# Asking for the next pair's norms before the first row chunk, and binding its transpositions behind scores, in the first batch of an attention and spectral-FFN kernel

## The chip, the cores and the metric

The kernel runs on one core of a Trainium2 chip. The metric is the time of one execution on the device in microseconds (us). The engines named below are TensorE (PE in the profile; PEld is its weight load), VectorE (DVE), ScalarE (ACT), GpSimd (POOL) and SyncE (SP), which only issues DMAs.

## The reference, cut to what matters

```python
def rmsnorm(x, g):                       # over head_dim = 64
    return x / np.sqrt(np.mean(x * x, -1, keepdims=True) + 1e-6) * g
q_n, k_n = rmsnorm(q, g_q), rmsnorm(k, g_k)
scores = (q_n @ k_n.T) / np.sqrt(64)     # 8 batches, 12 heads, 448 rows
attn = softmax(scores); out = attn @ v   # float32
x = out.transpose(0, 2, 1, 3).reshape(8, 448, 768)
u = x + np.real(fft(fft(x, axis=1), axis=2))
un = (u - mean(u)) / sqrt(var(u) + 1e-6)
return u + np.maximum(un @ w_ch1, 0) @ w_ch2   # 768 -> 3072 -> 768
```

The weights w_ch1 and w_ch2 come as 64-bit floats and are turned into pairs of 32-bit parts on the chip, in the first batch.

## The kernel before, in words

A batch has three stages: attention, the spectral part, and the feed-forward network (FFN). From batch 0's FFN on, the attention of the next batch is laid beside the FFN's matmuls. The first batch has no FFN to lie beside, so from the start to its own FFN, TensorE has only attention, spectral work and small transpositions; ScalarE and VectorE have softmax, copies out of PSUM, and the conversion of weights (lines 838 to 865, names `magw1e`, `dblw1e`, `w1e`, and the same with 2).

Attention goes through six pairs of heads (lines 585 to 620). In a trace or an order, `S_p_c_h` is the score tile of pair p, row chunk c (four chunks of 112 rows) and head h of the pair. For each pair:

- Norms (`norm_pair`, line 309): ScalarE squares q and k of the pair into the tile `qkn`, VectorE sums into `ss`, GpSimd raises `ss` to the power -1/2 and then multiplies q and k by it, one instruction each. The tile `qkn` has one buffer.
- Transpositions (`transpose_pair`, line 355): four matmuls against `ident` turn q (`qk_p_0`), four turn k (`qk_p_1`). ScalarE copies the results to `QT` and `KD`.
- Scores and softmax (`softmax_pair`, line 413): per chunk and head one matmul at line 439 whose operands have 64 rows; head 0 uses rows 0 to 63 of the array, head 1 rows 64 to 127. VectorE takes the minimum of the tile (`mn`), ScalarE the exponential (`P`) with the row sum. Even chunks use the two PSUM banks of tag `S`, odd chunks those of tag `ffn`. The transposed q of the next pair uses a bank of tag `S` too (line 215).
- Values (`value_pair`, `value_halves`): `P` is turned (`rem`, `pt`), copied by ScalarE (`R`, `T`) and multiplied with `v` (`av`); `spread` turns the row sums.

`attention` is a generator. While pair p's four chunks are asked for, it also asks for steps of the pair before (values) and of the pair after (`ahead`). Before the change the norms of pair p+1 are asked for behind chunk 1, its q behind chunk 2, its k behind chunk 3. Each yield also is a step for the caller (lines 1162 to 1169): every step adds 0.12 of a weight conversion (`CONVERT_EARLY`), step 40 loads the constants of the DFT, and steps 112 to 126 start batch 1's attention.

What is asked for is not yet the order on an engine. A scheduler sorts each engine's queue by the order of asking and by its own model of when operands and buffers are ready, and an engine runs its queue in that order. Two instructions of one engine can be tied by `order(...)` with the class NoSync, which sets their order in the queue and no semaphore.

```python
ahead = transpose_pair(*next_pair(b, p))        # line 594
for i in range(4):
    yield next(rows)                            # scores and softmax of chunk i
    for _ in range(2):
        yield next(values, 0)
    if i >= 1:
        yield next(ahead, 0)                    # line 600
```

Of the kernel before, what the change touches and what calls it, by code (L numbers as in the profile page):

```python
# [92 lines left out]
def spectral_block(ctx, tc, q, k, v, g_q, g_k, w1, w2, d1, d2, out, nb=B):  # L93
# [175 lines left out]
    def next_pair(b, p):  # L269
        return (b, p + 1) if p + 1 < NPAIR else (b + 1, 0)  # L270
# [70 lines left out]
        return qk, vhl  # L341

    ready = {}
    sums = {}
    freed = {}

# [8 lines left out]
    def transpose_pair(b, p):  # L355

        if b >= nb or (b, p) in ready:
            return
        load_pair(b, p)
        load_pair(*next_pair(b, p))  # L360
        qk, vhl = norm_pair(b, p)
        yield 0

        if plain_s(b, p):
            T = []
            for i, tag in enumerate(("QT", "KD")):
                pt = bank(QK_BANKS[b > 0][i], f"qk{b}_{p}_{i}")
                for c in range(NC):
                    rows = qk[i][:, c] if b + p == 0 else qk[:, i, c]
                    nc.tensor.transpose(  # L370
                        pt[:, c * C : (c + 1) * C],
                        rows.rearrange("t h d -> t (h d)"),
                        ident[:C, :C],
                    )
                t = sb.tile([128, S], F32, tag=tag, name=f"{tag}{b}_{p}")
                if i == 0:
                    A.copy(t, pt[:, :S])
                else:
                    A.activation(t, pt[:, :S], AF.Copy, scale=gneg)
                T.append(t)  # L380
                yield 420
            ready[b, p] = T[0], T[1], vhl
            return

        QT = sb.tile([128, 2, S], F32R, tag="QT", name=f"QT{b}_{p}")
        KD = sb.tile([128, 2, S], F32R, tag="KD", name=f"KD{b}_{p}")
        for i in range(2):
            pt = bank(QK_BANKS[b > 0][i], f"qk{b}_{p}_{i}")
            for c in range(NC):
                nc.tensor.transpose(  # L390
                    pt[:, c * C : (c + 1) * C], qk[:, i, c].rearrange("t h d -> t (h d)"),
                    ident[:C, :C],
                )
            src = pt[:, :S]
            if i == 0:
                A.copy(QT[lo, 0], src[lo])
                A.copy(QT[hi, 1], src[hi])
                sub(QT[hi, 0], src[lo], QT[lo, 0])
                sub(QT[lo, 1], src[hi], QT[hi, 1])
            else:  # L400
                for h, sl in enumerate((lo, hi)):
                    A.activation(KD[sl, h], src[sl], AF.Copy, scale=gneg[sl])
                    V.scalar_tensor_tensor(
                        out=KL[sl, h], in0=src[sl], scalar=gneg[sl], in1=KD[sl, h],
                        op0=ALU.mult, op1=ALU.subtract,
                    )
                A.copy(KD[hi, 0], KD[lo, 0].bitcast(F32))
                A.copy(KD[lo, 1], KD[hi, 1].bitcast(F32))
            yield 420

        ready[b, p] = QT, KD, vhl

    def softmax_pair(b, p, Pc):
        QT, KD, _ = ready[b, p]
        if b == 0:
            sums[b, p] = sb.tile([C, NC, 2], F32, tag="sums", name=f"sums{b}_{p}")
        for c in range(NC):
            P = slot("P", f"P{b}_{p}_{c}")[:C, : 2 * S]
            Ph = [P[:, :S], P[:, S:]]
            mn = sb.tile([C, 2], F32, tag="mn", name=f"mn{b}_{p}_{c}", bufs=4)  # L420
            if b == 0:
                sm = sums[b, p][:, c]
            else:
                sm = sb.tile([C, 2], F32, tag="sm", name=f"sm{b}_{p}_{c}", bufs=4)
            cs = slice(c * C, (c + 1) * C)
            tag = "ffn" if b == 0 and c % 2 else "S"
            banks = [bank(tag, f"S{b}_{p}_{c}_{h}")[:C, :S] for h in range(2)]

            def together(mm):
                if plain_s(b, p) and b and tag in freed:  # L430
                    order(
                        mm, freed[tag],
                        mybir.DependencyClass.Sync, mybir.DependencyReason.SCHED_ONLY,
                    )

            for h, s_ in enumerate(banks):
                hs = (lo, hi)[h]
                if plain_s(b, p):
                    mm = nc.tensor.matmul(  # L439
                        s_, QT[hs, cs], KD[hs], start=True, stop=True  # L440
                    )
                    if h == 0:
                        together(mm)
                    continue
                for step, K in enumerate((KD, KL)):
                    nc.tensor.matmul(  # L446
                        s_, QT[:, h, cs], K[:, h], start=step == 0, stop=step == 1
                    )
            for h, s_ in enumerate(banks):
                V.tensor_reduce(mn[:, h : h + 1], s_, axis=AX.X, op=ALU.min)  # L450
                scale = -1.0
                if b + p == 0:
                    n = 2 * c + h
                    scale = scales[:, 0, 8 + n : 9 + n]
                    V.tensor_tensor(
                        out=mn[:, h : h + 1], in0=mn[:, h : h + 1],
                        in1=scales[:, 0, n : n + 1], op=ALU.mult,
                    )
                freed[tag] = A.activation(
                    Ph[h],  # L460
                    s_,
                    AF.Exp,
                    bias=mn[:, h : h + 1],
                    scale=scale,
                    accum_out=sm[:, h : h + 1],
                )
            if b == 0:
                Pc.append(P)
                yield 760
                continue  # L470
            A.activation(sm, sm, AF.Identity, bias=tiny[:C])
            V.reciprocal(sm, sm)
            for h in range(2):
                if b < EARLY and h == 0:
                    A.activation(Ph[h], Ph[h], AF.Copy, scale=sm[:, h : h + 1])
                    continue
                V.tensor_scalar(
                    out=Ph[h], in0=Ph[h], scalar1=sm[:, h : h + 1], scalar2=None,
                    op0=ALU.mult,
                )  # L480
            Pc.append(P)
            yield 760
# [102 lines left out]
    def attention(b, xT, EO):  # L585
# [3 lines left out]
        for p in range(NPAIR):  # L589
# [2 lines left out]
            Pc = []  # L592
            rows = softmax_pair(b, p, Pc)
            ahead = transpose_pair(*next_pair(b, p))
            for i in range(4):
                yield next(rows)
                for _ in range(2):
                    yield next(values, 0)
                if i >= 1:
                    yield next(ahead, 0)  # L600
# [608 lines left out]
```

## Time and profile before

| | us |
|---|---|
| median of three runs | 2119.1 (2118.2 to 2119.41) |
| the profiled execution | 2117.71 |
| its span, first to last instruction | 2115.9 |
| TensorE busy in the span | 2069.7 |
| VectorE, ScalarE, GpSimd busy | 1512.3, 1111.9, 200.1 |
| mean granted TensorE clock | 0.985 |

Times in the trace count from the span's start. The granted clock is a share of full speed; 1.00 is 2.4 GHz and 0.50 is 1.2 GHz. The page's line of 40 slices shows TensorE at nine tenths or more in all slices but the first three and one near the end, so the places to look at are at the beginning. The share of busy time alone doesn't say who is waited for: a matmul that waits for another engine shows as idle time before it, with its releaser. Matmuls at line 439 are recorded twice each, so that x4 is two of them; transpositions are recorded once, so that x4 is the four chunks of one tile.

### The profile page before, as it was taken

To read this page: it belongs to the slowest core of one execution; us is meant where nothing else is said; L and a number is where in the kernel's file an instruction comes from. 1 tells how busy PE (TensorE), PEld (TensorE's weight loads), DVE (VectorE), ACT (ScalarE), POOL (GpSimd) and SP (SyncE) were. 2 spreads that over 40 slices of the span, in tenths; PEclk is the share of its full clock that TensorE was granted. 3 is DMA by queue.
4 is the path that set the end of the run, shared out by engine and by line. 5 is a ranking of instruction groups with operands and counts; after the bars stand their busy time and mean duration, and the time that the engine had idled before them with its cause. 6 is when DMAs were issued, how large, how long until landed. Compare 5 with 4: busy or idle time off the path is not lost.

```text
span 2115.9 us, 31172 instructions
## 1 busy us (share of the span) xinstructions
PE 2069.7 (98%) x11282; PEld 1812.0 (86%) x11282; DVE 1512.3 (71%) x2890; ACT 1111.9 (53%) x2437; POOL 200.1 (9%) x112
## 2 busy tenths in 40 slices
PE   8889999999999999999999999999999999998999
PEld 3347777999999999999999999999999999997998
DVE  6798989877875788667885778757786678743122
ACT  7878886555634666256642666436652566422100
POOL 3321110010100110000010011001100001000000
PEclk7989999999999999999999999999999999999999
DMA  7565978676556745585565855567465765459664
GB/s 235 165 208 173 330 247 288 241 223 186 173 176 202 223 150 172 181 246 172 173 196 172 238 175 170 183 199 223 158 173 178 237 185 157 166 167 278 195 218 151
DMA packets 294493, 422.11 MB, mean 199 GB/s; under 512 B 182994, under 2 KB 221315, under 8 KB 294340
## 3 DMA queue, kind: packets, MB, share of 16 engines
q1 hardware_dynamic: 293252, 419.43, 64.6%
q8 instruction: 90, 1.47, 0.3%
q10 hardware_dynamic: 1088, 0.69, 0.1%
q14 instruction: 63, 0.52, 0.1%
HBM read 360.27 MB, written 65.28 MB: 201 GB/s over the span
## 4 chain that ended last, share of the span: by engine, by line
PE 87%; DVE 4%; ACT 4%; DMA 2%; issue 2%; POOL 1%; SPq 0%; ACTq 0%; DVEq 0%; POOLq 0%
PE o L1109 31%; PE h L1088 31%; PE S L446 6%; PE av L574 4%; PE pt L562 4%; PE y L705 2%; PE S L439 1%; PE qk L390 1%; PE x L737 1%; ACT P L116 1%; DMA u_dram<-u 1%; PE av L508 1%; PE oT L1021 1%; PE pt L500 1%; PE ab L793 1%
## 5 line engine op out<-in xcount | busy, mean ns | idle before, releaser
L1109 PE MATMUL o<-hs,w 128*128 128x448 f32 x3420 | 774.0, 370 | 3.7 <-DMA w<-w 3.1
L1088 PE MATMUL h<-unT,w 128*128 128x448 f32 x3402 | 767.5, 370 | 2.1 <-DMA w<-w 1.5
L1109 PEld LDWEIGHTS o<-hs,w 128*128 128x128 f32 x3420 | 632.2, 189 | 57.9 <-issue 6.2
L1088 PEld LDWEIGHTS h<-unT,w 128*128 128x128 f32 x3402 | 627.5, 188 | 59.2 <-issue 7.9
L116 ACT ACTIVATE P<-S,mn 112x448 f32<-112x448 f32 x376 | 238.7, 637 | 186.6 <-DVE mn L116 182.2
L116 DVE TENSOR_REDUCE mn<-S 112x1 f32<-112x448 f32 x384 | 234.9, 618 | 55.0 <-PE S L446 36.1
L116 ACT ACTIVATE hs<-h 128x448 fp32r<-128x448 f32 x192 | 104.3, 543 | 298.5 <-PE h L1088 297.3
L116 POOL TENSOR_TENSOR ss<-ss,nhalf 112x16 f32<-112x16 f32 x47 | 143.1, 3044 | 1117.2 <-DVE ss L116 1022.6
L116 DVE SCALAR_TENSOR_TENSOR hs<-h,hs 128x448 fp32r<-128x448 f32 x192 | 119.2, 621 | 147.5 <-ACT hs L116 146.3
L116 DVE TENSOR_TENSOR acc<-o,acc 128x448 f32<-128x448 f32 x240 | 148.1, 619 | 91.7 <-PE o L1109 90.4
L116 ACT CAST T<-pt 128x448 fp32r<-128x448 f32 x216 | 113.4, 531 | 94.1 <-PE pt L562 92.0
L116 DVE TENSOR_TENSOR T<-pt,T 128x448 fp32r<-128x448 f32 x216 | 132.4, 620 | 36.5 <-ACT T L116 35.1
L574 PE MATMUL av<-T,vhl 128*128 128x448 f32 x432 | 153.2, 385 | 0.0
L116 DVE TENSOR_SCALAR P<-P,sm 112x448 f32<-112x448 f32 x312 | 129.0, 451 | 4.8
L562 PE MATMUL pt<-ident,P 112*128 112x112 f32 x864 | 121.7, 259 | 0.0
L562 PEld LDWEIGHTS pt<-ident,P 112*128 112x128 f32 x864 | 102.7, 140 | 16.5
L446 PE MATMUL S<-KD,QT 128*112 128x448 f32 x288 | 110.1, 382 | 0.0
L446 PE MATMUL S<-rounded,QT 128*112 128x448 f32 x288 | 105.4, 366 | 0.0
L574 PEld LDWEIGHTS av<-T,vhl 128*128 128x128 f32 x432 | 80.8, 188 | 6.7
L116 POOL TENSOR_TENSOR rstd<-st,nhalf 112x1 f32<-112x1 f32 (+2 forms) x32 | 20.3, 635 | 602.1 <-DVE st L116 602.1
L116 ACT ACTIVATION_READ_ACCUMULATOR P<-S,mn 112x1 f32 x376 | 74.8, 199 | 0.0
L439 PE MATMUL S<-KD,QT 64*112 64x448 f32 x192 | 67.0, 667 | 7.6 <-ACT P L116 4.1
(156 smaller groups left out, 2433.9 us busy)
## 6 DMA issues: line engine op xcount, KB each, us to landing
w<-w SPq DMA_DIRECT2D x285, 512.0 KB
w<-w SPq DMA_DIRECT2D x189, 768.0 KB
dblw<-w SPq DMA_DIRECT2D x30, 512.0 KB
dblw<-w SPq DMA_DIRECT2D x15, 768.0 KB
raw<-k SPq DMA_DIRECT2D x96, 112.0 KB
raw<-q SPq DMA_DIRECT2D x96, 112.0 KB
v<-v SPq DMA_DIRECT2D x96, 96.0 KB
u_dram<-u SPq DMA_DIRECT2D x24, 336.0 KB
```

Of the source, the lines that this page charges most:

```text
L116: ins = emit(*args, **kwargs)
L390: nc.tensor.transpose(pt[:, c * C : (c + 1) * C], qk[:, i, c].rearrange("t h d -> t (h d)"), ident[:C, :C],)
L439: mm = nc.tensor.matmul(s_, QT[hs, cs], KD[hs], start=True, stop=True)
L446: nc.tensor.matmul(s_, QT[:, h, cs], K[:, h], start=step == 0, stop=step == 1)
L500: nc.tensor.transpose(pt[:, c * C : (c + 1) * C], piece, ident[:C, :C])
L508: mm = nc.tensor.matmul(av[a, :S], v_[:, j, h], T[h], start=j == 0, stop=False)
L562: nc.tensor.transpose(pt[:, c * C : (c + 1) * C], Pc[c][:, 512 * h + j * 128 : 512 * h + (j + 1) * 128], ident[:C, :C],)
L574: nc.tensor.matmul(av[:, :S], lv, T[:, i], start=(j == 0 and i == 0), stop=False)
L705: nc.tensor.matmul(o, src[:, par, t0 : t0 + n], D1[:, ri, par, cols], start=i != 1, stop=i != 0,)
L737: nc.tensor.transpose(xp[:n, i * 128 : (i + 1) * 128], src[:, 3 * half + i], ident)
L1088: pace(nc.tensor.matmul(o, w[:, a, c], unT[c][:, z], start=n == 0, stop=n == 17))
L1109: mm = nc.tensor.matmul(o, w[:, a, f], hs[4 * g + f][:, z], start=n == 0, stop=n == 11)
```

## The change

In the first batch the generator of the next pair is asked for one step more, ahead of the current pair's first chunk. So the norms are asked for before chunk 0, q's transpositions behind chunk 1, and k's behind chunk 2. The first of each four transpositions is tied behind the score matmul that was asked for last at that moment (`scored[0]`): for q the last one of chunk 1, for k the last one of chunk 2. This holds for pairs 1 to 5 of the first batch and pair 0 of the second. Each pair of the first batch has one yield more.

```diff
@@ -341,6 +341,7 @@
     ready = {}
+    scored = [None]
     sums = {}
@@ -367,11 +368,16 @@
                 for c in range(NC):
                     rows = qk[i][:, c] if b + p == 0 else qk[:, i, c]
-                    nc.tensor.transpose(
+                    turned = nc.tensor.transpose(
                         pt[:, c * C : (c + 1) * C],
                         rows.rearrange("t h d -> t (h d)"),
                         ident[:C, :C],
                     )
+                    if c == 0 and scored[0] is not None and b * NPAIR + p <= NPAIR:
+                        order(
+                            turned, scored[0], mybir.DependencyClass.NoSync,
+                            mybir.DependencyReason.DATA,
+                        )
@@ -439,6 +445,8 @@
                     mm = nc.tensor.matmul(
                         s_, QT[hs, cs], KD[hs], start=True, stop=True
                     )
+                    if b == 0:
+                        scored[0] = mm
                     if h == 0:
                         together(mm)
@@ -592,6 +600,8 @@
             rows = softmax_pair(b, p, Pc)
             ahead = transpose_pair(*next_pair(b, p))
+            if b == 0:
+                yield next(ahead, 0)
             for i in range(4):
```

The first place is TensorE's queue in the first pair of the first batch, from the second head of chunk 1 on. Before:

```order
7 L439 MATMUL S_0_1_1_189<-KD_0_164,QT_0_157 112x448
8 L439 MATMUL S_0_2_0_226<-KD_0_164,QT_0_157 112x448
9 L439 MATMUL S_0_2_1_227<-KD_0_164,QT_0_157 112x448
10 L543 MATMUL rem_0_293<-ident,P_0_0_174 128x112
11 L500 MATMUL pt_0_0_0_303<-ident,P_0_0_174 128x112
12 L370 MATMUL qk_1_1_255<-ident,qkn_1_203 128x112 x4
13 L439 MATMUL S_0_3_0_245<-KD_0_164,QT_0_157 112x448
14 L500 MATMUL pt_0_0_0_303<-ident,P_0_1_186 128x112
15 L439 MATMUL S_0_3_1_246<-KD_0_164,QT_0_157 112x448
16 L543 MATMUL rem_0_293<-ident,P_0_1_186 128x112
17 L370 MATMUL qk_1_0_236<-ident,qkn_1_203 128x112 x4
```

In the changed kernel the same place reads:

```order
7 L445 MATMUL S_0_1_1_202<-KD_0_164,QT_0_157 112x448
8 L371 MATMUL qk_1_0_224<-ident,qkn_1_178 128x112 x4
9 L551 MATMUL rem_0_306<-ident,P_0_0_187 128x112
10 L508 MATMUL pt_0_0_0_316<-ident,P_0_0_187 128x112
11 L445 MATMUL S_0_2_0_233<-KD_0_164,QT_0_157 112x448
12 L445 MATMUL S_0_3_0_252<-KD_0_164,QT_0_157 112x448
13 L508 MATMUL pt_0_0_0_316<-ident,P_0_1_199 128x112
14 L445 MATMUL S_0_3_1_253<-KD_0_164,QT_0_157 112x448
15 L551 MATMUL rem_0_306<-ident,P_0_1_199 128x112
16 L445 MATMUL S_0_2_1_234<-KD_0_164,QT_0_157 112x448
17 L371 MATMUL qk_1_1_243<-ident,qkn_1_178 128x112 x4
```

The transposed q of pair 1 moved ahead of chunk 2, the transposed k from ahead of chunk 3 to behind all scores, and the two heads of chunk 2, which were neighbours, now stand apart.

The second place is TensorE's queue in pair 3 of the first batch, where the k of pair 4 is turned. Before:

```order
110 L543 MATMUL rem_2_655<-ident,P_2_3_577 128x112
111 L370 MATMUL qk_4_1_791<-ident,qkn_4_720 128x112 x4
112 L439 MATMUL S_3_2_0_730<-KD_3_601,QT_3_575 112x448
113 L439 MATMUL S_3_2_1_731<-KD_3_601,QT_3_575 112x448
114 L439 MATMUL S_3_3_0_761<-KD_3_601,QT_3_575 112x448
115 L439 MATMUL S_3_3_1_762<-KD_3_601,QT_3_575 112x448
116 L508 MATMUL av_1_476<-T_1_0_2_594,v_1_275 64x448
```

In the changed kernel, rows of the same pair (the rest of `pt_2_0_0` and `pt_2_1_0` lies between the two pieces):

```order
110 L551 MATMUL rem_2_681<-ident,P_2_3_584 128x112
111 L445 MATMUL S_3_3_0_781<-KD_3_582,QT_3_551 112x448
112 L516 MATMUL av_1_495<-T_1_0_2_614,v_1_275 64x448
113 L516 MATMUL av_1_495<-T_1_1_2_621,v_1_275 64x448
114 L537 MATMUL av_1_495<-R_1_485,v_1_275 64x448 x2
115 L508 MATMUL pt_2_0_0_691<-ident,P_2_0_470 128x112
```

```order
119 L445 MATMUL S_3_3_1_782<-KD_3_582,QT_3_551 112x448
120 L508 MATMUL pt_2_1_0_708<-ident,P_2_0_470 128x112
124 L371 MATMUL qk_4_0_728<-ident,qkn_4_649 128x112 x4
125 L445 MATMUL S_3_2_0_737<-KD_3_582,QT_3_551 112x448
126 L528 MATMUL spread_2_717<-ident,sums_2_469 64x112 x8
133 L445 MATMUL S_3_2_1_738<-KD_3_582,QT_3_551 112x448
134 L371 MATMUL qk_4_1_772<-ident,qkn_4_649 128x112 x4
```

The turned k of pair 4 no longer stands ahead of the last four scores of pair 3; those four, which followed one another, now stand alone, each between other work. GpSimd's queue reads the same before and after.

## Rows read from the trace of the kernel before

**Rows 1.** Stretches of the span, first line the columns; busy us of each engine
```profile
core 0: us, PE busy (x) PEld busy (x) DVE busy (x) ACT busy (x) POOL busy (x), PEclk, DMA share, GB/s
18.18:42.07 23.89, 22.46 (x64) 9.15 (x63) 16.71 (x30) 18.13 (x40) 4.94 (x3) 0.50 0.76 220
42.07:62.55 20.48, 16.09 (x99) 8.11 (x100) 17.62 (x28) 18.60 (x42) 4.94 (x3) 1.00 0.63 199
62.55:76.20 13.65, 9.86 (x36) 4.09 (x34) 6.98 (x13) 8.09 (x21) 5.52 (x3) 0.63 0.62 209
76.20:107.60 31.40, 28.10 (x170) 13.07 (x166) 28.00 (x50) 28.02 (x66) 13.07 (x6) 1.00 0.47 141
107.60:170.30 62.70, 49.50 (x264) 29.95 (x262) 52.41 (x110) 46.87 (x106) 16.26 (x10) 0.81 0.64 191
170.30:2116.00 1945.70, 1932.30 (x10626) 1742.35 (x10624) 1380.34 (x2642) 982.30 (x2149) 144.19 (x73) 1.00 0.65 200
```

**Rows 2.** What TensorE waited for, 0 to 180 us: total, times, longest
```profile
PE qk L370 <- POOL qkn L116: 8.8, 4, 3.8
PE av L508 <- ACT T L116: 4.9, 6, 2.0
PE S L439 <- ACT P L116: 4.1, 5, 2.6
PE S L439 <- ACT KD L116: 3.2, 3, 1.3
```

**Rows 3.** TensorE in order of time, pairs 0 and 1: start, us, count, idle before
```profile
17.82 0.75 PE L370 MATMUL qk<-ident,qkn 112*128 112x112 f32 x4 [2.81 <-POOL qkn L116]
18.50 1.83 PE L439 MATMUL S<-KD,QT 64*112 64x448 f32 x2
...
22.65 0.95 PE L370 MATMUL qk<-ident,qkn 112*128 112x112 f32 x4
...
24.22 1.84 PE L439 MATMUL S<-KD,QT 64*112 64x448 f32 x4 [0.25 <-ACT QT L116]
27.24 0.45 PE L500 MATMUL pt<-ident,P 112*128 112x112 f32 x1 [1.18 <-ACT P L116]
...
35.71 1.76 PE L520 MATMUL spread<-ident,sums 112*64 112x112 f32 x16
...
39.17 1.76 PE L508 MATMUL av<-T,v 128*64 128x448 f32 x4
40.86 1.01 PE L500 MATMUL pt<-ident,P 112*128 112x112 f32 x4
...
44.72 1.76 PE L439 MATMUL S<-KD,QT 64*112 64x448 f32 x8 [1.17 <-ACT KD L116]
```

**Rows 4.** GpSimd in order of time, the norms of pair 1 and of pair 4
```profile
14.81 2.96 POOL L116 TENSOR_TENSOR qkn<-raw,ss 112x512 f32<-112x512 f32 x2
...
65.58 3.48 POOL L116 TENSOR_TENSOR ss<-ss,nhalf 112x16 f32<-112x16 f32 x1 [10.42 <-DVE ss L116]
69.14 2.04 POOL L116 TENSOR_TENSOR qkn<-raw,ss 112x512 f32<-112x512 f32 x2
```

**Rows 5.** TensorE in order of time, pair 3 and pair 4
```profile
66.89 0.55 PE L543 MATMUL rem<-ident,P 112*128 112x112 f32 x4
71.23 1.01 PE L370 MATMUL qk<-ident,qkn 112*128 112x112 f32 x4 [3.79 <-POOL qkn L116]
72.17 3.33 PE L439 MATMUL S<-KD,QT 64*112 64x448 f32 x8
...
92.53 1.00 PE L439 MATMUL S<-KD,QT 64*112 64x448 f32 x2
...
98.05 1.76 PE L439 MATMUL S<-KD,QT 64*112 64x448 f32 x8
```

**Rows 6.** VectorE in order of time, behind that wait
```profile
74.11 1.16 DVE L116 TENSOR_REDUCE mn<-S 112x1 f32<-112x448 f32 x2 [6.21 <-PE S L439]
```

**Rows 7.** Stretch 44 to 107.6 us: busy time, and shares in the chain of waits
```profile
44.00:107.60 63.60, 52.58 (x286) 24.01 (x286) 50.71 (x85) 52.78 (x123) 23.53 (x12) 0.92 0.56 177
...
by line: issue 16.2%; PE S L439 14.7%; ACT P L116 7.2%; PE av L508 6.1%; PE pt L500 5.9%; ACT T L116 5.4%; ACT magw1e L842 5.3%; PE av L529 4.2%; ACT magw2e L842 3.8%; POOL qkn L116 3.2%; PE qk L370 3.0%; DVE w1e L863 3.0%; DVE ss L116 2.7%
```

## The prediction

> **What bounds the kernel now.** I read the stretches first. From 170.3 us on, TensorE is busy for 1932.30 of 1945.70 us at full clock [rows 1]; nothing else can shorten that part by much, and the change touches none of its work. Before 170.3 us no engine is full: from 107.6 to 170.3 TensorE has 49.50 of 62.70 us, VectorE 52.41, ScalarE 46.87 [rows 1]. So the first batch up to its FFN is a web of waits, and whatever it gains or loses reaches the end nearly one for one, since a full queue of TensorE follows it. Next I read who is waited for: the largest item is 8.8 us for GpSimd's norm products ahead of the transpositions at line 370, in four waits [rows 2]. Two of the four are at the change's places: 2.81 us before 17.82 [rows 3] and 3.79 us before 71.23 [rows 5]. The other two, 2.2 us together, belong to pairs of the second batch, for which nothing is asked earlier. Last I read the granted clock: it is 0.50 (1.2 GHz) from 18.18 to 42.07 and 0.63 on average from 62.55 to 76.20 [rows 1], and both of the waits lie just ahead of or within such a time.
>
> **Part by part.** The sum is made against the profiled execution, 2117.71 us: a span of 2115.9 and 1.8 around it. The median of the runs shown is 1.4 above that.
>
> *The wait of pair 4 goes.* Before, four transpositions of k stand ahead of the last scores of pair 3 and wait until GpSimd ends at 71.2 [rows 4, 5]; behind them queue those scores, and VectorE idles 6.21 us for their first minimum [rows 6]. In the new order the norm chain doesn't start much sooner: the square still follows the copy to KD of pair 3 on ScalarE, since `qkn` has one buffer. But the transpositions stand later. From the first scores of pair 3 at about 61.7 there are now three slots of scores, three groups of `av`, two `pt`, `rem` and three lone heads ahead of `qk_4_0`, some 10 us or more, so it is asked for behind 71.2 and finds its data. What went: 3.79 us of idle time, and the slow clock behind it, 3.33 less 1.76 us for four scores (x8 at either clock) and about 0.46 of the 1.01 for the transpositions [rows 5], 5.8 in all. That is one end. The other: ScalarE was busy 52.78 of 63.60 us from 44 to 107.6 [rows 7], and where no such wait lies, from 76.2 to 107.6, it was busy 28.02 of 31.40, 89% [rows 1]. At that density 52.78 us of work need 59.2, 4.4 less than 63.60. I take -4.4, since that row is the same kind of work in the same kernel; the ends are 0 (ScalarE has another wait in its place) and -5.8.
>
> *Heads that stood side by side are split.* Two score matmuls of different heads use different halves of the array. Side by side both take 1.84 us at half clock (x4), and one alone takes 1.83 (x2) [rows 3]: a lone head pays for two. At full clock a run of four takes 1.76, 0.88 for a slot of two, and a lone head 1.00 [rows 5], so 0.12 more for a run of its own. In the order I count slots pair by pair: in pairs 0 and 1 they are 11 before and 11 after; in pairs 2 to 5 they are 5, 4, 5, 5 before and 6, 7, 7, 5 after, 19 against 25, in 13 runs against 18. The price is 6 x 0.88 + 5 x 0.12 = 5.9 us of TensorE. The cause is the banks: q's transposition now takes a bank of tag `S` ahead of chunk 2, so chunk 3 overtakes it and the two heads of chunk 2 come one by one. How much shows is bounded by 0 (TensorE idles 11.0 of 63.60 us there [rows 7]) and 5.9. In the chain of waits of that stretch, TensorE's lines of scores, values and transpositions hold 14.7 + 6.1 + 5.9 + 4.2 + 3.0 = 34% [rows 7]; that share of 5.9 is +2.0, which I take.
>
> The Trainium skill, "TensorEngine Tiling (Array Packing)", section "Key Properties", says that a change of tiling mode drains TensorE. The 0.12 us for a lone run agrees with a small price of that kind; if each of the five new runs paid it on both sides it would be 1.2 instead of 0.6, and the sum 0.2 later.
>
> *The first pair.* The norm of pair 1 stands where it stood on ScalarE, VectorE and GpSimd. TensorE now waits for it ahead of chunk 2, not behind it, but only for q: two products take 2.96 from 14.81, so q is there at 16.3 [rows 4], not 17.82. From 16.3, by the durations at half clock [rows 3]: `qk_1_0` with the two single transpositions 0.9; four lone heads and two single transpositions about 7.3; `qk_1_1` 0.95, two singles 0.6 and the copy to KD: scores of pair 1 start at 26.0 (before 24.22). Then three slots 5.3, two singles 0.6, a slot 1.76, `qk_2_0` 0.95, `pt` 1.0, `spread` 1.76, a slot 1.76, `qk_2_1` 0.95, `av` 1.76, and 1.5 for `pt` until the first scores of pair 2: 43.3, if nothing waits, and 45.9 with the 0.25, 1.18 and 1.17 that TensorE waited there before. It was 44.72. I take 0, with ends of -1.4 and +1.2.
>
> *The extra steps.* Six more yields bring 0.72 of a conversion forward, about 1.9 us of ScalarE by its three instructions, from the stretch after 107.6, where it is 75% busy, to the one before, where it is 83% [rows 1, 7]. I take 0 and keep -1.9 and +1.9. Loads of the next pair are issued with its norm; on SP's queue the four loads of pair 4 move ahead of one weight store, little else, and none of the waits above ends on such a load. Nobody is queued behind a new semaphore wait: the ties add order only.
>
> Sum: -4.4 + 2.0 + 0 + 0 = -2.4; 2115.3 for the profiled execution, **2116.7** as a median. Under 0.2%, 4.2 us, a measurement of this kernel can't tell a change from none.
>
> **The rivals.**
> *A, clearly faster.* The splits are all hidden, the wait's whole 5.8 comes, and the first pair gives 1.4: -7.2, 2111.9. Or the clock doesn't fall at 18.18, since TensorE resumes 1.5 us earlier: its 22.46 us of work at half clock would be 11.2, and ScalarE's 18.13 us at 89% would set 20.3 of the 23.89, -3.6 more: -6.0, 2113.1. For it: 11.0 idle us in the stretch. Against it: two lone heads of pair 0 still come first, and ScalarE is at 89% where nothing waits. Also the gap starts earlier, at the end of chunk 1, so it is as long as the one before.
> *B, slower.* Lone heads keep the slow clock. For it: from 18.18 to 42.07 TensorE was busy 22.46 of 23.89 us, much of it heads alone, and stayed at 0.50; it rose only after `av` and transpositions [rows 1, 3]. The new order has 24 lone heads, twelve before. If the half clock lasts 10 us into pair 2, the 79% busy of that stretch [rows 1] costs 7.9 more less 2.1 of idle, 5.8; with the splits fully exposed (+5.9) and -4.4 that is +7.3, 2126.4. It decides from the point where the half clock lasts about 5 us longer there. Against it: pair 1 in the new order has its chunks 2 and 3 side by side again before that time.
> *C, the change does no more than exchange waits.* The wait for the norm becomes one for `KD` or `P`, each up to 1.3 to 2.6 us now [rows 2]; gain and price cancel: 2119.1.
>
> **Chances.** The forecast with C, both within 0.2%: 0.44 (forecast 0.30, C 0.14). A 0.33. B 0.23. So faster 0.33, same 0.44, slower 0.23. The range from 2108 (a little below A with 1.9 of conversions) to 2126 (B) leaves out the long ends; the forecast's own range is 2113 to 2121.
>
> **What would show it.** Right: no wait of `qk` for GpSimd between 44 and 107 us; line 439 with some 6 us more busy time from 44 to 107 us; the first FFN matmul about 2.4 us before 170.3; the stretch behind it as long as before. Wrong: a clock of 0.50 beyond 42 us; a new wait of scores for `P` or `KD` of 3 us or more; a first FFN matmul moved by more than 5 us either way; or a difference that arises behind it, which I put at zero.

## The result

The changed kernel is slower: 2131.98 us (2129.5 to 2138.18, 4 runs) against 2119.26 us, a ratio of 1.0076, 95% interval 1.0064 to 1.0088. The forecast was 2116.7 us with a range up to 2126. The profiled execution took 2138.18 us, 20.5 more than that of before. It is the slowest of the four, so the places that are found in it below add up to more than the 12.7 us between the medians.

The same stretches as in [rows 1], in the changed kernel (us, then busy time of TensorE, its weight loads, VectorE, ScalarE and GpSimd, then granted clock, DMA share, GB/s):

```profile
18.18:42.07 23.89, 21.39 (x66) 9.10 (x64) 17.81 (x30) 15.74 (x33) 6.40 (x4) 0.59 0.78 222
42.07:62.55 20.48, 15.44 (x98) 8.07 (x96) 15.38 (x24) 17.67 (x44) 5.01 (x3) 1.00 0.54 170
62.55:76.20 13.65, 12.44 (x36) 4.03 (x36) 9.47 (x17) 10.49 (x25) 6.52 (x3) 0.72 0.53 172
76.20:107.60 31.40, 27.06 (x113) 13.64 (x114) 23.34 (x40) 20.19 (x47) 6.12 (x3) 0.66 0.59 175
107.60:170.30 62.70, 49.11 (x272) 27.53 (x268) 48.86 (x88) 43.39 (x100) 20.17 (x9) 0.85 0.51 157
```

The row to look at is 76.20 to 107.60. VectorE was busy 28.00 us there and ScalarE 28.02 [rows 1]; now it is 23.34 and 20.19, while TensorE, at a clock of 0.66 instead of 1.00, shows nearly the old busy time for two thirds of the matmuls (113 records instead of 170). Busy time at half clock is not work done; the count beside it says so.

Where the time is lost can be read from the first scores of each pair. Pair 3 starts at 62.61 (before 61.74), pair 4 at 88.24 (81.89), pair 5 at 112.51 (98.05 [rows 5]), and the first FFN matmul at 186.23 (170.32). So some 5.5 us arise in pair 3, 8.1 in pair 4, little from there to the FFN, and 4.4 more behind its start (from the first FFN matmul to the end 1950.0 us, before 1945.6). The first scores of pair 4, before, then in the changed kernel with those of pair 5:

```profile
81.89 1.76 PE L439 MATMUL S<-KD,QT 64*112 64x448 f32 x8
```

```profile
88.24 2.16 PE L445 MATMUL S<-KD,QT 64*112 64x448 f32 x6
...
112.51 1.77 PE L445 MATMUL S<-KD,QT 64*112 64x448 f32 x8 [0.68 <-ACT KD L116]
```

TensorE's waits up to 200 us (total, times, longest), to compare with [rows 2]:

```profile
PE qk L371 <- POOL qkn L116: 6.0, 3, 4.2
PE av L516 <- ACT T L116: 5.2, 5, 3.5
PE S L445 <- ACT P L116: 5.0, 6, 2.0
PE S L445 <- ACT KD L116: 3.3, 5, 1.0
PE h L1098 <- ACT unT L116: 3.2, 1, 3.2
...
PE qk L371 <- DVE xT L116: 2.8, 1, 2.8
```

The wait for GpSimd in pair 3 is gone, as meant. TensorE in order of time there, against [rows 5] (start, us, count, idle before):

```profile
66.73 0.41 PE L551 MATMUL rem<-ident,P 112*128 112x112 f32 x2 [0.93 <-ACT T L116]
...
68.63 1.83 PE L445 MATMUL S<-KD,QT 64*112 64x448 f32 x2
70.39 1.76 PE L516 MATMUL av<-T,v 128*64 128x448 f32 x4
72.08 1.76 PE L537 MATMUL av<-R,v 64*64 64x448 f32 x4
...
74.71 1.83 PE L445 MATMUL S<-KD,QT 64*112 64x448 f32 x2
...
77.28 0.95 PE L371 MATMUL qk<-ident,qkn 112*128 112x112 f32 x4
...
85.81 1.01 PE L371 MATMUL qk<-ident,qkn 112*128 112x112 f32 x4
...
95.42 0.97 PE L537 MATMUL av<-R,v 64*64 64x448 f32 x4
...
99.08 0.82 PE L508 MATMUL pt<-ident,P 112*128 112x112 f32 x4 [1.23 <-ACT R L116]
102.73 0.98 PE L371 MATMUL qk<-ident,qkn 112*128 112x112 f32 x4 [2.82 <-DVE xT L116]
```

The k and q of pair 4 find their data (no bracket at 77.28 and 85.81). But from 68.6 to 89 us TensorE works without a pause at half clock, four lone heads of 1.83 us among its work, and in pair 4 a new wait stands: 2.82 us for VectorE's `xT`. VectorE's queue ahead of it:

```profile
96.75 0.56 DVE L859 TENSOR_SCALAR magw1e<-magw1e 128x768 f32<-128x768 f32 x1
97.34 0.56 DVE L863 TENSOR_SCALAR magw1e<-magw1e 128x768 uint32<-128x768 uint32 x1
98.01 1.33 DVE L873 TENSOR_TENSOR w2e<-magw2e,w2e 128x512 fp32r<-128x512 f32 x1
99.27 1.79 DVE L867 SCALAR_TENSOR_TENSOR magw1e<-dblw1e,magw1e 128x768 uint32<-128x768 uint32 x1
101.09 0.96 DVE L871 CUSTOM_DVE_ANT_0 magw1e<-dblw1e,magw1e 128x1536 uint16<-128x1536 uint16 x1
101.97 0.62 DVE L116 TENSOR_TENSOR xT<-av,share 128x448 f32<-128x448 f32 x1
```

The `av` that `xT` adds ended at 96.39 (95.42 and 0.97); `xT` starts 5.6 us later, behind these five instructions of the conversion of weights. Before, the same addition started 0.17 us after its `av`:

```profile
92.14 0.63 DVE L116 TENSOR_TENSOR xT<-av,share 128x448 f32<-128x448 f32 x1 [0.17 <-PE av L529]
```

### The profile page after: what moved, and what is told of

Its sections match the earlier page's. It is cut to its first block, busy times and chain, and to the rows that moved or that the text cites. A ratio compares the mean times of both kernels' runs of the same rounds, so it can differ in the third digit from the quotient of the medians.

```text
span 2136.2 us, 31160 instructions
## 1 busy us (share of the span) xinstructions
PE 2083.6 (98%) x11282; PEld 1818.6 (85%) x11282; DVE 1516.5 (71%) x2890; ACT 1114.2 (52%) x2437; POOL 200.6 (9%) x112
## 4 chain that ended last, share of the span: by engine, by line
PE 89%; DVE 4%; DMA 3%; ACT 2%; issue 1%; SPq 1%; POOL 0%; ACTq 0%; DVEq 0%; POOLq 0%
PE o L1119 31%; PE h L1098 31%; PE S L454 5%; PE av L582 4%; PE pt L570 4%; PE S L445 2%; PE y L715 2%; PE av L516 1%; DMA w<-w 1%; PE qk L396 1%; PE pt L508 1%; PE x L747 1%; PE rem L551 1%; PE ab L803 1%; PE av L587 1%
## 5 line engine op out<-in xcount | busy, mean ns | idle before, releaser
L445 PE MATMUL S<-KD,QT 64*112 64x448 f32 x192 | 73.0, 675 | 8.6 <-ACT P L116 5.0
```

Of the source, the lines that this page charges most:

```text
L445: mm = nc.tensor.matmul(s_, QT[hs, cs], KD[hs], start=True, stop=True)
```

## The experiments

Each run is compared with the kernel before on the same chip, whose medians there were 2115.9 to 2117.0 us. The theories at first: H, the split heads; N, the early norms; Y, the extra steps. The edits act in the first batch.

| run | median us | ratio to before, 95% interval |
|---|---|---|
| changed, heads side by side (e1) | 2133.33 | 1.0081, 1.0063 to 1.0099 |
| changed, no extra step (e2) | 2123.56 | 1.0034, 1.0023 to 1.0045 |
| early norms, transpositions at old places (e3) | 2117.66 | 1.0003, 0.9994 to 1.0013 |
| ties alone (e4) | 2118.25 | 1.0007, 0.9998 to 1.0017 |
| before with extra steps alone (e5) | 2132.58 | 1.0084, 1.0067 to 1.0100 |
| changed, extra steps convert nothing (e6) | 2119.40 | 1.0016, 1.0006 to 1.0026 |
| changed, extra steps not counted (e7) | 2119.76 | 1.0016, 1.0004 to 1.0029 |
| as e2, heads side by side (e8) | 2124.96 | 1.0045, 1.0030 to 1.0060 |
| before, the three numbers moved (e9) | 2128.30 | 1.0061, 1.0046 to 1.0076 |
| changed, DFT_STEP 43 (e10) | 2124.56 | 1.0047, 1.0031 to 1.0064 |
| changed, AHEAD_FROM 118 (e11) | 2126.62 | 1.0056, 1.0041 to 1.0071 |
| before, CONVERT_EARLY 0.118 (e12) | 2119.89 | 1.0017, 1.0007 to 1.0028 |
| changed, pair 3 side by side (e13) | 2131.33 | 1.0071, 1.0043 to 1.0099 |
| changed, once more (e15) | 2133.94 | 1.0073, 1.0051 to 1.0094 |
| changed, three numbers put back (e16) | 2132.07 | 1.0070, 1.0053 to 1.0086 |
| before, 5 early conversions (e17) | 2111.78 | 0.9976, 0.9965 to 0.9987 |
| changed, 5 early conversions (e18) | 2119.80 | 1.0020, 1.0010 to 1.0031 |

**e1, heads side by side.** The tie that `together` makes is made in the first batch too:

```diff
-                    if plain_s(b, p) and b and tag in freed:
+                    if plain_s(b, p) and tag in freed:
```

> The changed kernel, with one more tie in the first batch: head 0 of a chunk waits until the banks of both heads are free, as the later batches do already. In the order the scores of the first batch then take 27 slots instead of 36, nearly all heads side by side; norms, transpositions and the extra yields stay early. Theory H (split heads make the loss: each takes a slot alone and keeps TensorE at 1.2 GHz): most of the 12.7 us go, 2115 to 2122, and the half clock from 68 to 89 us is gone or under 8 us long. Theory N (the early norms disturb ScalarE's and VectorE's queues): 2128 to 2134, as the changed kernel. Theory Y (the six extra yields bring weight conversions forward, VectorE's queue stalls): the same, 2128 to 2134.

2133.33: nothing came back with 27 slots of scores, so H falls. The waits moved instead: `av` waited 11.0 us for ScalarE's copies `T`.

**e2, no extra step.** The norm is asked for in the same place, without a yield:

```diff
             if b == 0:
-                yield next(ahead, 0)
+                next(ahead, 0)
```

> The changed kernel, but the early request of the norms is no step for the caller, so conversions, DFT constants and the second batch come at the steps they had before. 38 slots of scores in the first batch (the changed kernel 36, the one before 30). Theory H: still slow, 2127 to 2136. Theory N: still slow. Theory Y: back to 2117 to 2121.

2123.56, and with 38 slots, more than in the changed kernel. Half of the loss goes with the steps (a ratio of 1.0034 in place of 1.0076), the other half stays, less than Y expects to go.

**e3, norms early, transpositions late.** As e2, and the later steps of `ahead` stand where they stood:

```diff
                 if i >= 1:
-                    yield next(ahead, 0)
+                    yield next(ahead, 0) if b or i > 1 else 0
```

> The norms early as in the change, no extra yields, but the transpositions asked for behind chunks 2 and 3 as before, each tied behind the last scores asked for. 28 slots of scores. Theory H: no loss, 2112 to 2120, perhaps below the kernel before, since the waits for GpSimd go too. Theory N: slow, 2126 or more. Theory Y: not slow, 2119 or a little less.

2117.66: not to be told from before. Early norms do no harm, so N falls, and they bring nothing either. This run is also the one that takes the wait of pair 4 away: of the 3.79 us before [rows 5] there is 0.30 left,

```profile
71.30 0.60 PE L371 MATMUL qk<-ident,qkn 112*128 112x112 f32 x4 [0.30 <-POOL qkn L116]
```

and between 44 and 107 us `av` waits 4.8 us for ScalarE's `T`, where it waited 2.6 before. By its interval the gain is at most 0.06%, 1.3 us. (That the early norms cost what the wait's end brings is possible; no run has one without the other.) The step from here to e2, the transpositions asked for one chunk earlier, costs 5.9 us (2123.56 less 2117.66).

**e4, ties alone.** The early request is left out, the ties stay:

```diff
-            if b == 0:
-                yield next(ahead, 0)
```

> The kernel before with the ties alone: norms and transpositions asked for at the old places, the first of each four transpositions tied behind the last scores asked for. The scores keep their 30 slots; only the transposed k of pairs 1 and 4 moves behind the scores it stood ahead of. Theory H: 2112 to 2118, the 3.8 us wait and the slow clock behind it gone. Theories N and Y: within 2 us of 2119, or the same gain; they say nothing against it.

2118.25. TensorE's waits for `qkn` fall to 3.4 us in two (8.8 in four before [rows 2]), and the time doesn't move: `av` waits 6.3 us for `T` now (4.9 before). The wait of pair 4 is not gone here, though; it only stands behind the scores of pair 3 now, and is 1.2 us shorter:

```profile
70.27 1.01 PE L371 MATMUL qk<-ident,qkn 112*128 112x112 f32 x4 [2.58 <-POOL qkn L116]
```

So that taking this wait away is worth nothing rests on e3.

**e5, extra steps alone.** The kernel before with one empty step more in each pair:

```diff
             ahead = transpose_pair(*next_pair(b, p))
+            if b == 0:
+                yield 0
```

> The kernel before with nothing but one more empty step in each pair of the first batch: norms, transpositions and scores are asked for as before, and the order of TensorE's scores is nearly the old one (29 slots of scores against 30 before and 36 in the changed kernel). Theory Y (the six extra steps bring conversions of weights forward, and in the queues of ScalarE and VectorE these stand ahead of what the pairs wait for): the loss is there without the rest of the change, about 9 us, 2123 to 2130. Theory E (the extra steps cost only together with transpositions that are asked for one chunk earlier, since then both press on the same stretch): within 4 us of before, 2113 to 2121.

2132.58: a loss as large as the whole, with neither an early norm nor a tie in it, and scores in 29 slots. Theory E falls, and the loss is above what Y expects. It isn't lost at the same place, though. Of the 15.5 us that its span is longer, 8.3 arise ahead of the first FFN matmul (178.58) and 7.2 behind it; in the changed kernel these are 15.9 and 4.4. The rows for 44 to 107.6 and 107.6 to 170.3 us of this kernel:

```profile
44.00:107.60 63.60, 54.78 (x277) 24.95 (x277) 50.68 (x87) 51.71 (x121) 21.38 (x11) 0.85 0.60 180
107.60:170.30 62.70, 45.62 (x242) 27.14 (x242) 46.84 (x86) 38.99 (x87) 12.24 (x8) 0.80 0.51 157
```

Up to 107.6 it does about as much as before [rows 7]; its second part is the poor one, with ScalarE at 38.99 us where it was at 46.87 [rows 1].

A step of the first part does three things: it adds `CONVERT_EARLY` to the debt of conversions; its number decides at `DFT_STEP` when the constants of the transform are asked for; and its number decides from `AHEAD_FROM` to `AHEAD_UNTIL` when the second batch's first steps run. Counted in the program, the last step of the first part has the number 131 before and 137 in the changed kernel. No conversion is added by that: the list of the first part (`sweep`) holds fifteen, which fall due by step 125 in both kernels, and each trace shows fifteen, nine of `w1e` and six of `w2e`. In the changed kernel:

```profile
L852 ACT ACTIVATE magw1e<-dblw1e x9: 874/898/955, 13.5 to 150.8; 128x768 f32<-128x768 f32 x9
L852 ACT ACTIVATE magw2e<-dblw2e x6: 651/671/698, 75.3 to 160.5; 128x512 f32<-128x512 f32 x6
```

What moves is the place in the work at which each is asked for, by up to six steps. The next runs take the three things apart.

**e6 and e7, the two sides of a step.** In e6 the extra steps yield -1 and the loop converts only for other values; in e7 they convert but don't count:

```diff
-    for n, _ in enumerate(aux(0)):
+    for n, cost in enumerate(aux(0)):
...
-        if n:
+        if n and cost >= 0:
```

```diff
+    n = -1
+    for cost in aux(0):
+        if cost < 0:
+            convert_some(CONVERT_EARLY)
+            continue
+        n += 1
```

> The changed kernel, whose extra steps convert nothing (the share of conversions is not added in them), but still count, so that the transform's constants are asked for at the same step number and the second batch's first steps begin six steps earlier in the work. 38 slots of scores. Theory Yc (of the extra steps it is the conversions that cost): about as the kernel without extra steps, 2119 to 2126. Theory Yn (it is the shifted counts: second batch's work and constants earlier): as the changed kernel, 2129 to 2135. Its pair (the next run) must come out the other way round under each.

> The changed kernel, whose extra steps convert as they do there, but are left out of the count, so that constants and the second batch's first steps come at their old places in the work. 35 slots of scores. Theory Yc (conversions): as the changed kernel, 2129 to 2135. Theory Yn (the shifted counts): 2119 to 2126.

2119.40 and 2119.76. They were to come out opposite; they lose only 3.4 and 3.8 us. So neither the conversions nor the counts make the loss alone; with the early transpositions it takes both. Nor do the prices add: each of the two has one side of the steps more than e2, and neither is slower than it (1.0016 against 1.0034). And e6 has 38 slots of scores, two more than the changed kernel. Its row for 44 to 107.6 us, and that of the changed kernel:

```profile
44.00:107.60 63.60, 59.95 (x320) 26.75 (x316) 55.05 (x92) 56.44 (x135) 22.05 (x12) 0.95 0.67 207
```

```profile
44.00:107.60 63.60, 53.92 (x236) 24.96 (x238) 47.17 (x77) 46.41 (x107) 17.65 (x9) 0.77 0.55 169
```

With as many lone heads, all three engines do more, and the clock is 0.95 instead of 0.77.

**e8, no extra step and side by side.** The edits of e1 and e2 together.

> The changed kernel without its extra steps and with the two heads of a chunk bound side by side: 27 slots of scores instead of 38 in the kernel without extra steps alone (2123.6). Theory H2 (what is left of the loss without extra steps, some 6 us, is the heads that come one by one): 2114 to 2119. Theory T (what is left comes from transpositions that are asked for one chunk earlier, and so from the order of the queues behind them, whichever way the heads stand): 2121 to 2128.

2124.96 with 27 slots, against 2123.56 with 38: H2 falls. What is left without the steps lies with the transpositions asked for one chunk earlier (e3 shows that the norms aren't it), and not with the lone heads that they make.

**e9, the places by numbers.**

```diff
-CONVERT_EARLY = 0.12
-DFT_STEP = 40
+CONVERT_EARLY = 0.1255
+DFT_STEP = 37
-AHEAD_FROM = 112
-AHEAD_UNTIL = 127
+AHEAD_FROM = 106
+AHEAD_UNTIL = 121
```

> The kernel before without any extra step; the three numbers of the step loop alone are set so that what they place stands where six extra steps would place it: CONVERT_EARLY 0.1255 (16 conversions in the first part, as with extra steps, against 15), DFT_STEP 37, AHEAD_FROM 106 and AHEAD_UNTIL 121. Theory P (the loss of 13 to 17 us is where conversions, constants and the second batch's first steps stand; the steps themselves are nothing): 2128 to 2136. Theory S (the extra steps act by something else, such as the points at which the program's generators take turns): within 4 us of before, 2113 to 2121.

2128.30, 12.4 us slower without any extra step, at the lower edge of what P expects. There is no sixteenth conversion here either; the trace has fifteen, only earlier. Moving what the steps place is enough for three quarters of what e5 loses.

**e10 and e11, constants or second batch.**

```diff
-DFT_STEP = 40
+DFT_STEP = 43
```

```diff
-AHEAD_FROM = 112
-AHEAD_UNTIL = 127
+AHEAD_FROM = 118
+AHEAD_UNTIL = 133
```

> The changed kernel with DFT_STEP 43, so that the constants of the transform are asked for at the old place in the work; conversions and the second batch's steps stay early. Theory D (the constants, which stood three steps earlier within pair 2, are what makes conversions collide with pair 3): 2118 to 2124. Theory A (the second batch's steps are the partner of the conversions): 2128 to 2135.

> The changed kernel with AHEAD_FROM 118 and AHEAD_UNTIL 133, so that the second batch's first steps come at their old place in the work; conversions and the transform's constants stay early. Theory A: 2118 to 2124. Theory D: 2128 to 2135. If both this run and the one with the old place of the constants come out near 2120, or both near 2132, neither is the partner by itself.

2124.56 and 2126.62: each gives back part (ratios 1.0047 and 1.0056 against 1.0076), e7 with both at old places 1.0016. Neither D nor A alone.

**e12, a small move.**

```diff
-CONVERT_EARLY = 0.12
+CONVERT_EARLY = 0.118
```

> The kernel before with CONVERT_EARLY 0.118 in place of 0.12: still 15 conversions in the first part, each at most two steps later. It asks how far a small move of conversions, with nothing else changed, moves the time. Theory R (this part of the kernel answers to any small move of its order with some us, since the order was chosen by time for one setting): over 4 us away from before on either side, most likely slower, 2120 to 2130. Theory O (only large moves or an added conversion matter): within 2 us of before, 2114 to 2119.

2119.89, 3.95 us slower (0.07 to 0.28%). By the program's count one conversion comes three steps later and the others at most two. So small a move shifts this kernel by as much as e6 and e7 differ from before; some 4 us can't be given a cause of their own here. Beyond what O allows and at R's edge.

**e13, side by side in pair 3 alone.**

```diff
-                    if plain_s(b, p) and b and tag in freed:
+                    if plain_s(b, p) and (b or p == 3) and tag in freed:
```

> The changed kernel with the two heads of a chunk bound side by side in pair 3 alone: 5 slots of scores there instead of 7, and TensorE's order is that of the changed kernel up to that pair. Theory C (lone heads of pair 3 hold the half clock there from 68 to 89 us, which costs some 6 to 9 us): the clock is back at 1.00 within 8 us of its fall, and 2122 to 2127. Theory Q (the queues of ScalarE and VectorE set the end, and TensorE's clock there is only a follower): 2129 to 2135.

2131.33 (2127.62 to 2139.01), above what C expects, so the heads of pair 3 don't cost 6 to 9 us. In its profile, one of its faster executions (2128.15), the half clock ends by 76 us and pair 4 starts at 81.4; but e15 below shows the same without the edit. A gain of a few us can't be excluded by this interval. The `xT` of pair 4 starts 0.1 us behind its `av` here (92.94), and TensorE doesn't wait for it.

**e14, the clock beside lone heads.** The matmuls have 112 columns of weights and move 448, each recorded twice; `gap` lets VectorE copy ten times before the next series. Ahead of the kernel before's work:

```diff
+        heads(whole, 24)
+        heads(one, 24)
+        gap()
+        heads(one, 30)
+        gap()
+        heads(pair, 30)
+        gap()
+        heads(whole, 30)
```

> The kernel before with a series of matmuls of a head's size ahead of its work: 24 of 112 columns on all 128 rows, 24 of one head alone (64 rows); then, each behind a pause of about 5 us in which VectorE copies, 30 of one head alone, 30 pairs of heads side by side, and 30 on all rows. Its time is not compared. Theory C (one head alone leaves the clock low): it falls within the first series of lone heads, or after a pause stays at 0.50 for the lone heads (30 x 0.9 = 27 us or more) and comes back for the pairs and for all rows. Theory W (only waits lower it): 1.00 in the lone series without a pause, and behind each pause the same short time at 0.50 whichever way the heads stand.

TensorE in order of time, then three stretches with the clock (third column from the end):

```profile
8.31 36.42 PE L1164 MATMUL warmed<-warm 128*112 128x448 f32 x96
...
50.34 0.31 PE L543 MATMUL rem<-ident,P 112*128 112x112 f32 x1 [2.15 <-ACT P L116]
...
50.80 22.80 PE L1164 MATMUL warmed<-warm 64*112 64x448 f32 x60
78.47 1.09 PE L1164 MATMUL warmed<-warm 64*112 64x448 f32 x1 [4.87 <-DVE warm L116]
```

```profile
50.80:73.60 22.80, 22.80 (x60) 10.30 (x60) 0.00 (x0) 1.08 (x2) 0.00 (x0) 1.00 0.00 0
78.47:83.80 5.33, 5.33 (x14) 2.33 (x16) 0.00 (x0) 0.00 (x0) 0.00 (x0) 0.50 0.01 3
83.80:95.00 11.20, 11.20 (x62) 5.33 (x60) 0.00 (x0) 0.00 (x0) 0.00 (x0) 0.98 0.00 0
```

The first row holds 24 matmuls on all rows and 24 lone heads (shown as one). 24 and 30 lone heads in a row keep 1.00; the clock is 0.50 behind the pause of 4.87 us, and back after 5.3 us of pairs. Since other work lay in the first pause, the lone heads behind it met no half clock, so whether they would hold it longer than pairs do wasn't seen. That a row of lone heads lowers it by itself, as C has it, is ruled out.

**e15, the changed kernel once more.** No edit.

> The changed kernel once more, for a second profile and a ratio on this chip. If the slow stretch in pairs 3 and 4 belongs to the kernel's order, its clock is again about 0.50 from 69 to 89 us and the time 2129 to 2138. If it belongs to one execution, the clock there is mostly 1.00 and the profiled execution some 5 to 9 us shorter than 2138, while the median stays.

2133.94. In this profile the clock falls at 69 us too and is back at 75, but it falls again at 98:

```profile
68.95 1.83 PE L445 MATMUL S<-KD,QT 64*112 64x448 f32 x2
...
75.03 1.00 PE L445 MATMUL S<-KD,QT 64*112 64x448 f32 x2
...
98.08 0.98 PE L371 MATMUL qk<-ident,qkn 112*128 112x112 f32 x4 [3.06 <-DVE xT L116]
98.99 1.83 PE L445 MATMUL S<-KD,QT 64*112 64x448 f32 x2
```

Pair 4 starts at 83.4 us here, 4.8 earlier than in the first profile; the execution is 1.4 us shorter (2136.77). That the half clock lasts 20 us in pair 3 belongs to one execution, and what it costs is mostly given back later. The half clock in sum doesn't: in both executions it begins at the same two places, the scores behind `rem` in pair 3 and the wait for `xT` in pair 4, and the mean clock from 44 to 107.6 us is 0.77 in the first profile and 0.80 here, against 0.92 before [rows 7]:

```profile
44.00:107.60 63.60, 52.99 (x245) 23.78 (x242) 47.32 (x78) 46.34 (x108) 18.29 (x9) 0.80 0.59 185
```

The wait for `xT` belongs to the kernel: 2.82 and 3.06. So does pair 4: 25.7 us from its first score to that of pair 5 here (109.06 less 83.41), 24.3 in the first profile, 16.2 before.

**e16, the numbers put back.** The changed kernel with

```diff
+CONVERT_EARLY = 0.1148
+DFT_STEP = 43
+AHEAD_FROM = 118
+AHEAD_UNTIL = 133
```

> The changed kernel, extra steps included, with the three numbers of the step loop set so that what they place stands at its old place in the work: CONVERT_EARLY 0.1148 (15 conversions), DFT_STEP 43, AHEAD_FROM 118 and AHEAD_UNTIL 133. Theory P (placement): as the kernel without extra steps, 2119 to 2126. Theory S (the steps by themselves): 2129 to 2136.

2132.07: no gain, as S expects and against P, while e9 came out for P. The same three things stand within a step or two of where e2 has them, and the time is 8.5 us longer (1.0070 against 1.0034). It looks like the answer of e12 on a larger scale, that neither "earlier" nor "later" names the difference; no run shows that. And the `xT` of pair 4 isn't late here. It starts 0.1 us behind its `av`, which ended at 91.20, TensorE has no wait for it, and the loss is the same:

```profile
91.28 0.62 DVE L116 TENSOR_TENSOR xT<-av,share 128x448 f32<-128x448 f32 x1
```

**e17 and e18, fewer conversions.** CONVERT_EARLY 0.04 in the kernel before, 0.0385 in the changed one:

> The kernel before with CONVERT_EARLY 0.04: 5 conversions in the first part instead of 15, so that ScalarE and VectorE have some 10 x 1.6 and 10 x 3 us less to do ahead of the FFN; the rest of the conversions falls into the FFN. Its own time may lie on either side of before (2110 to 2125); it is there to be compared with the next run.

> The changed kernel with CONVERT_EARLY 0.0385, which makes 5 conversions in its 138 steps too. Theory V (conversions that stand ahead of what the pairs wait for are the vehicle of the loss): at most 5 us slower than the kernel before with 5 conversions. Theory G (the stage answers to any new order, and the order before was the best of many): 8 us or more away from it, on either side.

2111.78 and 2119.80, 8.0 us apart: about half of the changed kernel's loss is there with a third of the conversions. That is more than V allows and at G's edge. The two rows for 44 to 107.6 us, e17 first (the profile of e18 is of its slowest execution, 2125.06):

```profile
44.00:107.60 63.60, 56.55 (x347) 27.58 (x345) 44.23 (x74) 50.34 (x122) 19.32 (x10) 0.97 0.42 120
```

```profile
44.00:107.60 63.60, 61.18 (x309) 27.94 (x309) 40.71 (x69) 46.10 (x114) 17.49 (x10) 0.87 0.34 95
```

In e18 TensorE is the full engine, 61.18 of 63.60 us, for fewer matmuls. Here, with ScalarE and VectorE relieved, 35 slots of scores against 31 and a clock of 0.87 against 0.97 are what is left to pay; that the slots make the 8 us was not tried apart.

e17 also beats the kernel before, by 0.13 to 0.35%: the best version found.

## Why the prediction was wrong, step by step

**The extra steps: the step that failed.** I wrote: "Six more yields bring 0.72 of a conversion forward ... I take 0 and keep -1.9 and +1.9." Alone they cost 16.6 us (e5, 2132.58 less 2115.99); taken out of the changed kernel they give back some 8 (e2). Two things were wrong with it. The step number also places the constants and the second batch's first steps, and I priced neither; without the counts the changed kernel gives back most of its loss (e7), as it does without the conversions (e6). And I priced the work that moves (ScalarE's time for it) and not the order of the queues that it moves in. The work that moves is small, as I had it: no conversion is added, and up to 107.6 us the changed kernel has finished ten, before nine. What the new order does to a queue is seen in one place, the `xT` that starts 5.6 us late behind five instructions of conversions. That place is not the loss as a whole: e13 and e16 lose as much without it.

**The wait of pair 4, -4.4.** The wait went as described, and so did its sign, no wait of `qk` for GpSimd between 44 and 107 us. Its worth was 0, the end of its range that I had not taken: e3 leaves 0.30 us of it and measures 1.0003 (0.9994 to 1.0013), with more waits of `av` for `T` in its place. ScalarE's density of 89% was no limit that the rest would move up to.

**Split heads, +2.0.** That a lone head costs a whole slot stands: in e14 it takes 0.76 us (22.80 for 30) and a pair of heads as long. But it isn't the loss: fewer slots bring no gain clear of the noise (e1, e8, e13), and with 38 slots e6 is 3.4 us slower than before in all. The transpositions asked for earlier, which split the heads, do cost 5.9 us without the steps (e2 less e3), and as much when the heads stand side by side (e8). The sum had no term for that.

**The first pair, 0.** Right: q's transposition ran at 16.73 (16.3 forecast), the first scores of pair 2 stood at 44.06, within 43.3 to 45.9.

**Behind the FFN's start, 0.** 4.4 us arise there, 5.2 in e15, 7.2 in e5 and 0.3 in e1; not settled.

**Rival B, slower at 2126.4 by a slow clock with lone heads in pair 2.** The time went its way but not by its mechanism. Pair 2 ran at 1.00; the slow clock came in pairs 3 and 4, and lone heads keep 1.00 (e14). Nor is a lower clock the loss: at an equal mean clock of the whole execution the changed kernel is some 13 us slower, 2132.66 us at 0.982, 2130.18 at 0.983 and 2129.50 at 0.984, where the executions of before with these clocks average 2119.4, 2117.3 and 2115.5. Within one kernel the clock and the time go together (2138.18 at 0.979), so it may have a part in the spread of its executions. A and C fall with the time, though an exchange of waits, as C has it, is what e3 shows.

**What is shown, and what stays open.** Shown: the loss has two sources in the program, the extra steps (half of it, e2; as much as all of it when they come alone, e5) and the transpositions asked for one chunk earlier (the other half, e2 against e3); early norms and ties alone lose nothing that can be measured (e3, e4); of the steps, neither the conversions nor the counts make the loss alone (e6, e7); and with a third of the conversions about half of the loss remains (e17, e18). One route on the engines is seen in both traces of the changed kernel, conversions ahead of `xT` in pair 4, and runs without it lose as much. Not settled: why putting the three numbers back brings nothing (e16) while taking the steps out brings some 8 us (e2), and so which instructions make up the loss; the cause on the engines stays open. The e12 run suggests that every small reordering has a price of some us here, and that the numbers of the kernel before are a good draw among such orders; that is argued from the runs, not shown.

## What to carry to other kernels

When a generator's yields also drive other work, a new yield is an edit of all that work: list everything that counts steps before costing it. Price a moved instruction by what stands behind it in its queue too, not by its own time alone. Before crediting a removed wait, look whether the engines around it have spare time that another wait won't take; in a web of waits the first run should remove that wait alone.

## What the runs showed of the hardware

- TensorE's clock stayed at 1.00 through 54 lone heads. It was at 0.50 behind a pause of 4.87 us, and not behind one of 2.15 us (e14). In the changed kernel it fell at 68.6 us with no wait over 0.93 us in the 15 us ahead, and at the same instruction in e15 (68.95), which I can't explain.
- VectorE's instructions with two operands in SBUF took nearly twice as long beside GpSimd's product: 1.33 us instead of 0.69 and 1.79 instead of 0.95, while `qkn` ran:

```profile
97.43 2.81 POOL L116 TENSOR_TENSOR qkn<-raw,ss 112x512 f32<-112x512 f32 x2
```

The same two took 1.33 and 1.79 in the second profile of that kernel. The Trainium skill, "SBUF — State Buffer", section "SBUF: two separate sides", says that such an instruction and a GpSimd operation that reads SBUF take one shared pair of ports, each for its whole length; the trace agrees in kind, with delays of 0.64 and 0.84 us beside GpSimd instructions of about 1.4 (2.81 for two; the two products of the norm before, at 71.07, took 2.04).
